# Gate and value of a SwiGLU block as one 2x2 block product by seven block multiplications, after thresholded attention

## The chip, the cores and the metric

The kernel runs on one core of one Trainium2 chip. The metric is the device time of one execution in microseconds (us). Work is spread over five engines with instruction streams of their own: TensorE (PE, matrix products; its weight loads are listed as PEld), VectorE (DVE), ScalarE (ACT), GpSimd (POOL) and SyncE (SP, which here only issues DMAs). Matrix products go to PSUM, which has 8 banks of 512 float32 columns on each of 128 partitions.

## What is computed

Eight batches with eight heads of 576 tokens and 64 channels each go through an attention that keeps only scores close to the row's maximum; then all 4608 rows of 512 channels go through a SwiGLU block of width 1536. Everything is float32 (the three weight matrices arrive as float64).

```python
def _attn_ref(q, k, v, tau):
    scale = 1.0 / np.sqrt(q.shape[-1])
    scores = scale * np.matmul(q, k.transpose(0, 1, 3, 2))
    thresh = np.max(scores, axis=-1, keepdims=True) - tau
    scores = np.where(scores >= thresh, scores, -1000000000.0)
    scores = scores - np.max(scores, axis=-1, keepdims=True)
    attn = np.exp(scores)
    attn = attn / (np.sum(attn, axis=-1, keepdims=True) + 1e-09)
    return np.matmul(attn, v)

def _moe_ref(x, w_gate, w_val, w_out):        # x: 4608 x 512
    g = x @ w_gate                            # 512 x 1536
    silu = g * (1.0 / (1.0 + np.exp(-g)))
    val = x @ w_val
    return silu * val @ w_out                 # 1536 x 512
```

## The kernel before

All of it is one instruction stream for each engine, in the order in which the Python code emits the instructions; each engine works its own list off strictly, and waits on the others where data demand it.

**Attention.** Work goes by segments: a pair of heads of one batch. A segment is cut into tiles of query tokens, four of 128 and one of 64 (`NT`); one such tile is a *slot*, so a batch is a block of 20 slots. Batch 0 is treated in a way of its own and is not touched in substance. From batch 1 on (`halved`), a slot runs so: PE writes two score tiles of two PSUM banks each (L345; one in the slot of 64 tokens; `ps_s` has two such tiles in all), DVE takes row maxima (`mx`, L368), exchanges them between partition groups (L318) and combines them (`nm`, L372), ACT computes the threshold (`th`, L383) and four exponentials into `pall` (L387), DVE masks and sums each (L391), ACT exchanges the sums (L321), DVE adds and inverts them (L406, L407), ACT and POOL scale two of the four pieces each (L399, L397), and DVE transposes them (L436). `turn(1)` leaves the newest scaled pieces lying, so that a transposition is emitted two slots after its scores. When the five slots of a segment are done, `attend` multiplies with `v` (L511) and ACT copies the result (`xa`) into the token buffer `xall` (L521, L528). The two arenas of `pall` in which successive segments put their exponentials overlap by two rows.

**SwiGLU.** Rows go through in units of 256 tokens: two of the first 512 tokens of each batch, and two that collect the last 64 tokens of four batches each, 18 in all. For each of 12 groups of 128 hidden columns, `rows_of_products` (L547) accumulates four products into `pg` (gate) and four into `pv` (value). ACT takes tanh and half of the gate (L560, L561), DVE and POOL make silu times value (L567, L579). The output product of the first two units is plain (L613); for the others `seven` (L645) treats it as a 2x2 block product (token halves by hidden halves times output halves) with seven block products instead of eight, with sums of weights (`ws2` to `ws4`) and of hidden blocks (`hs2`, `hs3`) made by POOL.

**Order.** PE interleaves both parts. `block()` is a generator that yields one matmul of the SwiGLU part at a time, and `fill(n)` draws n of them; `pace` sets how many each slot receives, so that the work left is spread evenly over the slots to come. In a slot come the scores, half of the share, the other half, and, in the second slot of a segment, the previous segment's `attend`. What is left after the last slot runs at the end with nothing beside it. q, k and v loads are issued on SP, output stores on POOL and at the end on SP.

Of the kernel before, what the change touches and what calls it, by code (L numbers as in the profile page):

```python
# [17 lines left out]

@with_exitstack
def kernel(  # L20
# [11 lines left out]

# [17 lines left out]
    XB = 5  # L68
# [7 lines left out]
    assert 2 * D == P and NCC == NP and D == 2 * G and S - SM == 2 * G and SM % TC == 0 and B % BT == 0 and QA == TC  # L76

    const = ctx.enter_context(tc.tile_pool(name="const", bufs=1))
    ld = ctx.enter_context(tc.tile_pool(name="ld", bufs=1))
    qkp = ctx.enter_context(tc.tile_pool(name="qkp", bufs=2))  # L80
    stp = ctx.enter_context(tc.tile_pool(name="stp", bufs=4))
    hp = ctx.enter_context(tc.tile_pool(name="hp", bufs=8))
    gp = ctx.enter_context(tc.tile_pool(name="gp", bufs=4))
    tp_ = ctx.enter_context(tc.tile_pool(name="tp", bufs=2))
    op = ctx.enter_context(tc.tile_pool(name="op", bufs=1))
    ps_s = ctx.enter_context(tc.tile_pool(name="ps_s", bufs=2, space=bass.MemoryType.PSUM))
    ps_f = ctx.enter_context(tc.tile_pool(name="ps_f", bufs=4, space=bass.MemoryType.PSUM))
    ctx.enter_context(tc.manual_schedule())


# [12 lines left out]
    vall = const.tile([P, 2 * NJ * D], F32, name="vall")  # L103


    NR = 2 * NT + 1
    pall = const.tile([P, 2 * NR - 2, S], F32, name="pall")

    free = NP * (S - TA * P)
    ident = pall.rearrange("p n s -> p (n s)")[:, free:free + P]  # L110
    make_identity(nc, ident)
    arenas = [pall[:, 0:NR, :], pall[:, NR - 2:, :]]

    ones = pall[:, 2 * NR - 4, 0:TC]
    nc.vector.memset(ones, 1.0)

    def run_idle(n):
        ps = ps_f.tile([P, 512], F32, name="idle", tag="psf")[:, 0:TC]
        for _ in range(n):
            nc.tensor.matmul(ps, ones[:, 0:P], ones, start=True, stop=True)  # L120

    wgv = const.tile([P, 2, NCC, DFF], F32, name="wgv")

    wo = const.tile([P, 2, NF, DM2], F32, name="wo")
# [4 lines left out]

    XW, HW = NCC * TC, NF2 * P  # L130
    xall = const.tile([P, XB * XW + 2 * HW], F32, name="xall")
    hs2, hs3 = (xall[:, XB * XW + n * HW:XB * XW + (n + 1) * HW].rearrange("p (f q) -> p f q", q=P)
                for n in range(2))


    extra = const.tile([P, 3 * NF2 * DM2], F32, name="extra")
    hfirst = extra[:, 0:NF * TC].rearrange("p (f n) -> p f n", n=TC)
    ws2, ws3, ws4 = (extra[:, n * NF2 * DM2:(n + 1) * NF2 * DM2].rearrange("p (f e) -> p f e", e=DM2)
                     for n in range(3))

# [4 lines left out]
    places += [xall[:, 3 * XW + n * 2 * TW:3 * XW + (n + 1) * 2 * TW] for n in range(2)]  # L156
    los = deque(extra[:, NF * TC + n * TW:NF * TC + (n + 1) * TW] for n in range(2))

    los.append(op.tile([P, 2, DM], F32, name="ob").rearrange("p i n -> p (i n)")[:, 0:TW])
# [66 lines left out]

    def load_qk(i):
        b, hp_ = divmod(i, NP)
        tiles = {}

        places_ = {1: extra[:, 0:2 * S], 2: extra[:, 2 * S:4 * S], 3: xall[:, XB * XW:XB * XW + 2 * S]}
        srcs = {"q": (q, "(j r) (e d) -> e r j d"),
                "k": (k, "(j r) (e d) -> e r j d" if b == 0 else "(r j) (e d) -> e r j d")}
        for x, name in enumerate("qk"):  # L240
            if i in places_:
                tiles[name] = places_[i][:, x * S:(x + 1) * S].rearrange("p (j d) -> p j d", d=G)
            else:
                tiles[name] = ld.tile([P, NJ, G], F32, name=f"{name}raw")
        raws = [tiles[name].rearrange("p j d -> p (j d)") for name in "qk"]
# [12 lines left out]
        if i < NP:  # L258

# [15 lines left out]

            own = xall[:, XB * XW + 2 * S:XB * XW + 3 * S - QA] if i == 0 else raws[0][:, QA:S]
# [7 lines left out]
        else:  # L284
            for name in "qk":
                load(name, slice(0, NJ), [nc.sync] * 2)
            if i == NP:
                scales.append(lambda: scale(raws[0]))
            else:
                scale(raws[0])  # L290
# [26 lines left out]
    def largest(out, in_):  # L317
        nc.vector.tensor_reduce(out=out, in_=in_, axis=AX.X, op=ALU.max)  # L318
# [665 lines left out]
```

## Time and profile before

| | us |
|---|---|
| three runs | 1507.58, 1509.18, 1509.38 |
| their median | 1509.18 |
| span of the profiled execution | 1509.0 |
| DVE busy in it | 997.8 |
| ACT busy | 726.6 |
| POOL busy | 642.1 |
| matmuls of gate, L547 `pg` (1728 records, two a matmul) | 403.9 |
| matmuls of value, L547 `pv` (1728 records) | 405.7 |
| matmuls of output, L645 (1344 records in three groups) | 311.5 |
| scores, L345 (4032 records) | 158.0 |
| attended product, L511 (2016 records) | 128.7 |
| POOL scaling, L397 | 265.4 |

The profile is of one execution. Busy time is the time in which at least one instruction of a group ran; matmuls overlap each other, so the price of one is read from the distance of their starts. A row of the timeline has the start, the duration up to the end of the last instruction of the row, the engine, the line, the operation with output and inputs, how many instructions are merged in it, and in brackets the idle time before it and what ended it. The mean clock granted to TensorE was 0.997 of full speed. DMA moved 66.93 MB, mean 44 GB/s.

### The profile page before, as it was taken

What the parts mean: (1) busy time and instruction counts of PE and PEld (TensorE: products, weight loads), DVE (VectorE), ACT (ScalarE), POOL (GpSimd) and SP (SyncE); (2) the same over time, 40 slices, a digit from 0 to 9 for tenths busy, and PEclk for the clock granted to TensorE, in tenths of its full rate; (3) what the DMA queues carried; (4) which work ended last, traced back from release to release, by engine and by line L of the source; (5) the groups of instructions that cost most, each with busy time, mean ns of one, the idle gap of its engine ahead of it and who ended that gap; (6) DMA issues with size and microseconds to landing.
All of it is one profiled execution on the core that took longest, in us unless ns stands there. A gap on an engine that the chain in (4) does not pass through costs nothing. (4 is left out here: it accounts for less than half of the span.)

```text
span 1509.0 us, 31516 instructions
## 1 busy us (share of the span) xinstructions
PE 1484.0 (98%) x11808; PEld 1124.8 (75%) x11808; DVE 997.8 (66%) x3040; ACT 726.6 (48%) x2158; POOL 642.1 (43%) x640
## 2 busy tenths in 40 slices
PE   9999899999999999999999999999999999999998
PEld 6677564477777777787777777777777777888887
DVE  7888887877777777737677666677666767412212
ACT  6887655555544545434545445454544554311110
POOL 2565543366453545435444444444545353500000
PEclk9999999999999999999999999999999999999999
DMA  7743211211111111112111011212110120000000
GB/s 176 194 152 88 69 33 43 50 33 33 46 33 47 33 43 23 39 22 46 33 40 21 20 46 33 46 33 47 33 43 11 40 48 16 1 14 1 15 15 14
DMA packets 177064, 66.93 MB, mean 44 GB/s; under 512 B 159888, under 2 KB 159888, under 8 KB 176912
## 3 DMA queue, kind: packets, MB, share of 16 engines
q1 hardware_dynamic: 170880, 56.62, 16.5%
q0 software_dynamic: 2432, 7.87, 1.4%
q8 instruction: 94, 1.54, 0.4%
q10 hardware_dynamic: 3600, 0.43, 0.2%
q14 instruction: 58, 0.48, 0.1%
HBM read 55.44 MB, written 9.44 MB: 43 GB/s over the span
## 5 line engine op out<-in xcount | busy, mean ns | idle before, releaser
L397 POOL TENSOR_SCALAR pall<-pall,ri 128x288 f32<-128x288 f32 (+1 forms) x260 | 265.4, 1030 | 345.3 <-DVE ri L407 328.2
L547 PE MATMUL pv<-xall,wgv 128*128 128x256 f32 x1728 | 405.7, 383 | 3.6 <-ACT pall L465 3.6
L547 PE MATMUL pg<-xall,wgv 128*128 128x256 f32 x1728 | 403.9, 383 | 0.7 <-ACT pall L465 0.7
L547 PEld LDWEIGHTS pv<-xall,wgv 128*128 128x128 f32 x1728 | 324.6, 190 | 69.3 <-issue 22.3
L547 PEld LDWEIGHTS pg<-xall,wgv 128*128 128x128 f32 x1728 | 324.1, 190 | 66.3 <-issue 22.0
L368 DVE TENSOR_REDUCE mx<-sc 128x2 f32<-128x576 f32 x252 | 180.7, 750 | 239.5 <-PE sc L345 238.5
L391 DVE SCALAR_TENSOR_TENSOR pall<-sc,th,pall 128x288 f32<-128x288 f32 (+1 forms) x540 | 258.0, 528 | 27.6 <-ACT pall L387 27.6
L387 ACT ACTIVATE pall<-sc,nm 128x288 f32<-128x288 f32 (+1 forms) x540 | 236.5, 510 | 0.6
L383 ACT ACTIVATE th<-nm,cut 128x4 f32<-128x4 f32 (+1 forms) x140 | 41.6, 297 | 386.1 <-DVE nm L372 386.1
L579 POOL TENSOR_TENSOR ht<-ht,gt 128x512 f32<-128x512 f32 x84 | 107.0, 1274 | 191.6 <-DVE ht L567 107.4
L436 DVE STREAM_TRANSPOSE pall<-pall 128x576 f32<-128x576 f32 x252 | 181.3, 754 | 2.8 <-POOL pall L397 2.8
L645 PE MATMUL po<-wo,ht 128*128 128x256 f32 x768 | 177.5, 381 | 0.0
L345 PE MATMUL sc<-kT,qT 64*32 64x288 f32 x4032 | 158.0, 411 | 12.2 <-DVE pall L391 10.9
L645 PEld LDWEIGHTS po<-wo,ht 128*128 128x128 f32 x768 | 144.6, 190 | 26.4 <-issue 6.0
L567 DVE SCALAR_TENSOR_TENSOR ht<-tn,pv 128x512 f32<-128x512 f32 x102 | 69.9, 685 | 132.3 <-PE pv L547 119.1
L399 ACT ACTIVATE pall<-pall,ri 128x288 f32<-128x288 f32 (+1 forms) x264 | 132.8, 553 | 0.0
L321 ACT COPY sums<-sums 32x4 f32<-32x4 f32 (+1 forms) x560 | 108.4, 194 | 50.0 <-DVE pall L391 38.8
L560 ACT ACTIVATE tn<-pg 128x512 f32<-128x512 f32 x108 | 64.8, 600 | 139.8 <-PE pg L547 133.0
L511 PE MATMUL xa<-pall,vall 64*64 64x288 f32 x2016 | 128.7, 405 | 0.0
L345 PEld LDWEIGHTS sc<-kT,qT 64*32 64x32 f32 x4032 | 58.8, 105 | 89.5 <-issue 60.9
L511 PEld LDWEIGHTS xa<-pall,vall 64*64 64x64 f32 x2016 | 74.3, 133 | 50.7 <-ACT sums L321 3.6
L663 POOL TENSOR_TENSOR ht<-ht,xall 128x256 f32<-128x256 f32 x48 | 34.1, 729 | 156.3 <-PE po L645 155.1
(114 smaller groups left out, 1336.5 us busy)
## 6 DMA issues: line engine op xcount, KB each, us to landing
vall<-in_v_dram SPq DMA_DIRECT2D x112, 144.0 KB, 3.4
kraw<-in_k_dram SPq DMA_DIRECT2D x114, 72.0 KB, 2.7
qraw<-in_q_dram SPq DMA_DIRECT2D x112, 72.0 KB, 2.4
out_dram<-ob POOLq DMA_DIRECT2D x28, 256.0 KB, 2.6
wo<-in_moe_w_gate_dram SPq DMA_DIRECT2D x16, 384.0 KB, 3.8
wo<-in_moe_w_val_dram SPq DMA_DIRECT2D x16, 384.0 KB, 4.4
xall<-in_moe_w_out_dram SPq DMA_DIRECT2D x5, 768.0 KB, 5.1
wo<-in_moe_w_out_dram SPq DMA_DIRECT2D x3, 768.0 KB, 6.3
```

The costliest lines, as they stand in the source:

```text
L321: nc.scalar.copy(out, in_[:, :, 0])
L345: nc.tensor.matmul(ps[g * G:(g + 1) * G, h, 0:SH], qT[hs, col + a * G:col + (a + 1) * G], kT[hs, c * SH:(c + 1) * SH], start=True, stop=True)
L368: nc.vector.tensor_reduce(out=mx[:, 2 * x:2 * x + 2, 0], in_=tile_[:, :, 0:SH], axis=AX.X, op=ALU.max, negate=True)
L387: nc.scalar.activation(ps[x], scs[x], AF.Exp, bias=nm[:, x:x + 1])
L391: nc.vector.scalar_tensor_tensor(out=ps[x], in0=scs[x], scalar=th[:, x:x + 1], in1=ps[x], op0=ALU.is_ge, op1=ALU.mult, accum_out=sm[:, x, ...
L397: nc.gpsimd.tensor_scalar(out=ps[x], in0=ps[x], scalar1=ri[:, x:x + 1], scalar2=None, op0=ALU.mult)
L399: nc.scalar.activation(ps[x], ps[x], AF.Copy, scale=ri[:, x:x + 1])
L436: nc.vector.transpose(out=p, in_=p)
L511: nc.tensor.matmul(xa[a][h * D:(h + 1) * D, at:at + n * G].rearrange("d (i q) -> d i q", q=G), vr[rs, h, j, :], p[rs, lo:lo + n, j, :], st ...
L547: nc.tensor.matmul(ps[:, i], wgv[:, mat, c, (f + i) * P:(f + i + 1) * P], x[:, c, cs], start=(c == 0), stop=(c == NCC - 1))
L579: eng.tensor_tensor(out=hts[x], in0=hts[x], in1=gt, op=ALU.mult)
L645: nc.tensor.matmul(ps, h(f), w[:, f, :], start=(f == 0), stop=(f == NF2 - 1))
```

## The change

**The product.** Gate and value of 512 tokens are taken as one block product. The token matrix is cut into two halves of 256 tokens by two halves of 256 channels, x11, x12, x21, x22; the weights for one group of 256 hidden columns into w11 (value, first channels), w12 (gate, first), w21 (value, second), w22 (gate, second). With

- s1 = x21 + x22, s2 = s1 - x11, s4 = x12 - s2, s3 = x11 - x21
- t1 = w12 - w11, t2 = w22 - t1, t4 = w21 - t2, t3 = w22 - w12

the seven products are p1 = x11 w11, p2 = x12 w21, p5 = s1 t1, p6 = s2 t2, p3 = s4 w22, p7 = s3 t3 and p4 = x22 t4, and value and gate of both halves are sums of these. Each is four matmuls of 256 columns (two groups of 128 hidden columns by two of 128 channels). A group of 256 hidden columns thus takes 28 matmuls in place of 32, and there are six such groups (`Group(c, g)`).

- Where two products are summed, PE writes the later one on into the same PSUM bank. Where a sum is used twice, ACT copies the bank in between (`cb`, `s5`, `u1`, `u2`); p2 waits for the copy of p1, p7 for that of p6, p4 for that of p7, p3 for that of p5. Gate sums are finished by DVE (`g1`) and POOL (`g2`).
- The sums of weights t1, t2, t4 are made once by POOL in block 1 and stored in DRAM (`sums_hbm`); `ring` holds two groups of them, and each group of each chunk is loaded again (`load_sums`, 768 KB, on SP) after p4 of two groups before. t3 takes the place of w12 in `wgv`. Slot 0 of the ring also serves as `hs2` and `hs3` of the output, so that its next load follows the fifth output product of a chunk's second half.
- Chunk 0 (batch 0) stays plain. Chunks 1 to 7 are the first 512 tokens of the other batches, chunk 8 collects the last 64 tokens of all batches, which go through DRAM (`last_hbm`).
- Four PSUM banks are handed out by name (`take`, `Hold`); at the end, when no scores run, four more.

**The order.** From batch 1 on, PE's order is a fixed table. Slots are numbered kk = 0 to 19 in a block; `GV` says how many of the 41 products of gate and value (the last p4 comes in slot 16) and `CH` how many of the 14 output products follow the scores of a slot. The table holds for blocks 2 to 7; in block 1 the plain work is shared out. `attend` of the previous segment comes in the third slot of a segment (kk = 2, 7, 12, 17), right behind the scores, ahead of the slot's other work.

The other engines' order follows from `Plan`: each piece of work is a `Job` with an engine, an estimated duration, a rank and what it depends on; when PE's next piece is emitted, all jobs that by the estimate have begun by then are emitted, for each engine the ready one of lowest rank first. A transposition (rank 2) is emitted when its scaled pieces are estimated to be ready, now one instruction of 1152 columns for a slot, where two of 576 were. Output stores go to SP.

In the built program, the exponentials of the slot with `attend` stand behind four ACT copies of `attend`'s result (L1210, L1211), and they write a part of `pall` that `attend` reads. DVE's transposition of a slot stands in most slots between `nm` and the first mask of the next slot.

```diff
+class Plan:
+    def job(self, eng, took, fn, *deps, rank=1, lag=0.0):
...
+                    n = min((i for i, j in enumerate(jobs) if j.ready <= start), key=lambda i: (jobs[i].rank, jobs[i].ready, i))
...
+    def pe(self, took, fn, *deps):
+        self.force(*deps)
+        for d in deps:
+            if d is not None:
+                self.t = max(self.t, (d.end if isinstance(d, Job) else d) + self.HOP)
+        self.run(self.t)
+        fn()
+        self.t += took
+        return self.t + self.PIPE
...
-            for f in range(0, NF, GR):
-                if f == EARLY:
-                    yield from late
-                yield from gate(j, cs, f, hts, gts)
-                if f >= EARLY:
-                    next(sums, 0)
-                yield from value(j, cs, f, hts, gts)
...
+    def weight_sums(g, s, *deps):
+        t1, t2, t4 = (ring_part(s, n) for n in range(3))
+        w11, w12, w21, w22 = pair_cols(wval, 0, g), pair_cols(wgat, 0, g), pair_cols(wval, 1, g), pair_cols(wgat, 1, g)
+        j = job("POOL", 1.3, pool_tt(t1, w12, w11, ALU.subtract), *deps, rank=3)
+        j = job("POOL", 1.3, pool_tt(t2, w22, t1, ALU.subtract), j, rank=3)
+        j = job("POOL", 1.3, pool_tt(t4, w21, t2, ALU.subtract), j, rank=3)
+        stores[g] = job("SP", 0.1, lambda: nc.sync.dma_start(out=sums_hbm[g], in_=ring[:, s]), j, lag=4.0)
...
+        def mul(self, hold, w, x, first, *deps):
+            def fn():
+                ps = hold.rows()
+                for i in range(2):
+                    for k_ in range(2):
+                        nc.tensor.matmul(ps[:, i], w[:, k_, i * P:(i + 1) * P], x[:, k_, :], start=first and i == k_ == 0,
+                                         stop=True, skip_group_check=True)
+            return pe(4 * MM, fn, *deps)
...
+        def p5(self):
+            m = self.mul(self.e, self.ring_w(0), xs[0], True, loads[self.c, self.g], ready_x[self.c][1], *self.e.deps)
...
+            self.s5 = job("ACT", 0.55, lambda: nc.scalar.activation(s.ap, self.e.rows(), AF.Copy, scale=0.5), m, *old, rank=0)
...
+        def p7(self):
+            m = self.mul(self.b, pair_cols(wgat, 0, self.g), x_block(self.c, 1, 0), False, self.u1, ready_x[self.c][3])
+            u, old = turn_of(u_bufs)
+            self.u2_buf = u
+            self.u2 = job("ACT", 0.55, lambda: nc.scalar.activation(u.ap, self.b.rows(), AF.Copy, scale=0.5), m, *old, rank=0)
+            tt, eng, took = (dve_tt, "DVE", 0.62) if tail[0] else (pool_tt, "POOL", 1.3)
+            self.g2 = job(eng, took, tt(u.ap, u.ap, self.s.ap, ALU.add), self.u2, self.s5, rank=1)
...
+        def p4(self):
+            m = self.mul(self.b, self.ring_w(2), x_block(self.c, 1, 1), False, self.u2)
+            self.finish(1, self.u2_buf, self.g2, self.b, m)
+            if self.g + 2 < NF2:
+                load_sums(self.c, self.g + 2, m)
...
+        for a in range(R):
+            def copy(a=a):
+                nc.scalar.copy(xk[:, a], holds[a].ap()[:, lo:lo + 2 * NT * G].rearrange("p (t i q) -> p t i q", t=2, q=G))
+                nc.scalar.copy(xl[:, a], holds[a].ap()[:, at_last:at_last + G])
+            js.append(job("ACT", 0.65, copy, m, last_store[0] if cc == 0 else None, rank=0))
...
+        seg["turned"].append(job("DVE", 0.72 * len(pss), lambda: nc.vector.transpose(out=whole, in_=whole), *scaled, rank=2))
...
+            new.p1(tail[0] or g in (0, 1, 3, 5))
+            yield
+            if old is not None:
+                old.p4()
+                yield
+            for fn in (new.p5, new.p2, new.p6, new.p3, new.p7):
+                fn()
+                yield
...
+    GV = {3: 4, 4: 3, 5: 4, 6: 4, 7: 1, 8: 4, 9: 2, 10: 4, 11: 3, 12: 1, 13: 4, 14: 3, 15: 4}
+    CH = {17: 1, 18: 3, 19: 2, 0: 3, 1: 2, 2: 1}
+    SHARES = [4.0, 4.0, 1.4, 4.0, 3.0]
...
+            pss, marks = slot_scores(seg, t)
...
+            if x == 2 and n > 0:
+                after = attend(halved[n - 1])
+                prepare_v(seg, after)
...
+            slot_rest(seg, t, pss, marks, after)
```

## The prediction

> **What bounds the kernel now.** I read the page's busy shares first, then busy time by stretches, then TensorE's timeline at the end, then all engines in one attention slot, then the DMA table. The share of each engine, and two stretches (columns: busy us and instructions of PE, PEld, DVE, ACT, POOL, then granted clock, DMA share, GB/s):
>
> ```profile
> PE 1484.0 (98%) x11808; PEld 1124.8 (75%) x11808; DVE 997.8 (66%) x3040; ACT 726.6 (48%) x2158; POOL 642.1 (43%) x640
> ```
>
> ```profile
> 180.00:190.00 10.00, 9.70 (x76) 6.88 (x77) 8.22 (x29) 5.85 (x18) 4.18 (x4) 0.83 0.41 88
> ...
> 420.00:580.00 160.00, 160.00 (x1380) 121.58 (x1383) 118.39 (x388) 82.33 (x260) 78.51 (x82) 1.00 0.17 38
> ```
>
> PE is busy without a gap from about 300 us on; DVE 74% and POOL 49% in the second stretch. So PE work that is removed comes out of the span one for one, until another wait opens. The price of that work is read at the end, where nothing else runs on PE (two records for each matmul):
>
> ```profile
> 1340.11 3.62 PE L547 MATMUL pg<-xall,wgv 128*128 128x256 f32 x16
> 1343.57 3.62 PE L547 MATMUL pv<-xall,wgv 128*128 128x256 f32 x16
> 1347.02 3.62 PE L547 MATMUL pg<-xall,wgv 128*128 128x256 f32 x16
> ```
>
> Groups of 16 records, 8 matmuls, start 3.453 us apart: 0.4316 us a matmul.
>
> Next the lags inside one attention slot:
>
> ```profile
> 803.81 4.59 PE L511 MATMUL xa<-pall,vall 64*64 64x288 f32 x72
> ...
> 808.34 1.20 PE L345 MATMUL sc<-kT,qT 64*32 64x288 f32 x32
> 808.44 0.77 ACT L521 COPY xall<-xa 128x128 f32<-128x128 f32 x4 [3.95 <-PE xa L511]
> 809.07 0.56 ACT L528 COPY xall<-xa 64x32 f32<-64x32 f32 x4
> 809.16 1.42 DVE L368 TENSOR_REDUCE mx<-sc 128x2 f32<-128x576 f32 x2 [6.12 <-PE sc L345]
> ...
> 811.65 1.43 DVE L436 STREAM_TRANSPOSE pall<-pall 128x576 f32<-128x576 f32 x2
> ```
>
> ```profile
> 799.70 1.65 ACT L387 ACTIVATE pall<-sc,nm 128x288 f32<-128x288 f32 x4
> ...
> 800.61 0.52 DVE L391 SCALAR_TENSOR_TENSOR pall<-sc,th,pall 128x288 f32<-128x288 f32 x1 [0.52 <-ACT pall L387]
> 801.05 0.08 DVE L391 DVE_READ_ACCUMULATOR pall<-sc,th,pall 128x1 f32 x1
> 801.05 0.51 DVE L391 SCALAR_TENSOR_TENSOR pall<-sc,th,pall 128x288 f32<-128x288 f32 x1
> ```
>
> ```profile
> 248.37 0.51 DVE L391 SCALAR_TENSOR_TENSOR pall<-sc,th,pall 128x288 f32<-128x288 f32 x1
> ...
> 249.04 0.72 PE L345 MATMUL sc<-kT,qT 64*32 64x288 f32 x16 [0.34 <-DVE pall L391]
> ```
>
> To be read: the two score units of a slot take PE 1.13 us (808.34 to 809.47, where the next matmul starts), one alone 0.57. The attended product takes 4.53 and its first copy starts at once (0.1 us after). Exponentials follow each other every 0.41 us; the first mask starts 0.91 us after the first exponential, further masks every 0.44 us. A freed score tile lets PE start 0.16 us after the mask's end (248.88 to 249.04).
>
> **What is removed.** Counted in the built programs: gate and value fall from 1728 matmuls of 256 columns to 192 plain (chunk 0) and 8 x 168 = 1344. That is 192 fewer, at 0.4316: -82.9 us. All other PE work keeps its counts (2016 score, 1008 attended, 672 + 48 output matmuls). Nothing hides it on PE, so it is worth its full price.
>
> **What is added, off PE.** For each chunk: 4 sums of tokens and 6 sums of gates on POOL (1.27 us each by the row L579, 1274 ns at the same shape), 12.7 us; 6 additions from PSUM on DVE (685 ns by L567), 4.1 us; on ACT 6 x 6 = 36 PSUM passes of 600 ns (rows L560, L561) for 24 before, +7.2 us. A block of 20 slots holds 42 x 1.726 (gate and value) + 84 x 0.4316 (output) + 36 x 0.57 + 4 x 4.53 = 147 us of PE work. POOL goes from 78 us in 160 to some 89 in 147 (61%), DVE to about 122 (83%), both beside PE: nothing by the sum. Weight sums (24 on POOL, six of these sets shipped out) lie in block 1 beside its plain work. The 48 reloads of weight sums, 768 KB each, are new SP issues; the same size now takes
>
> ```profile
> xall<-in_moe_w_out_dram SPq DMA_DIRECT2D x5, 768.0 KB, 5.1
> wo<-in_moe_w_out_dram SPq DMA_DIRECT2D x3, 768.0 KB, 6.3
> ```
>
> from issue to landing. A reload is issued when `p4` of a group ends and needed seven products later, 7 x 1.726 = 12.1 us, so it is hidden with 5.8 us to spare; queued ahead of it on SP are at most the eight q/k or four v loads of a slot. Only where the ring's slot 0 served as `hs2`, `hs3` is it close: two output products and one gate product, 6.9 us, in the two tail chunks. 0 to 2 us each; I take 1.0 each, 2 us.
>
> **What the new order costs PE.** This is the large unknown. The order of the built program shows three places (slots are numbered as in the table of the change).
>
> (1) The slot with `attend` (3rd of five). Its exponentials write where the attended product still reads, so they must wait for its end, T; and on ACT four copies stand ahead of them. Estimate from the rows: copies of 256 and of 32 columns issue about 0.29 + 0.14 us, twice: exponentials start at T + 0.95, masks at T + 1.86, the second mask ends at T + 2.81, PE may write that tile at T + 2.97. But the table gives PE only one product (1.73 us) after `attend` in slots 7 and 12, and one output product (2.59) in slots 2 and 17. PE stands 1.24 and 0.38 us. The second unit waits for the fourth mask, delayed by a PSUM pass of 0.5 us in slots 7 and 12 (T + 4.29) or an addition of 0.42 us (T + 4.27): another 0.75 and 0.73. So 2 x 1.99 + 2 x 1.11 = 6.2 us a block, 37 us in the six blocks 2 to 7. Before, the product stood at a slot's end, ahead of no exponential. Lower bound: first units alone, 3.2 a block, 19 us.
>
> (2) Slot 9 has one unit and two products, 4.1 us. Its masks come, by the same lags (reduction, exchange, 1.43 us transposition behind POOL's scaling, a PSUM pass among the exponentials), 4.5 to 6.6 us after its scores began, and slot 10's second unit needs them at 4.7. 0 to 1.9 us; I take 1.0: 6 us in six blocks (0 to 11).
>
> (3) Inside a group, PE writes on into a bank that ACT must first read. In 5 places of a chunk one product, 1.73 us, lies between; ACT needs 0.3 (lag of 1329.75 to 1330.01) + 0.6 and a lag back, 0.2 to 0.4. Hidden unless ACT is behind an exponential (0.41). 30 places at 0 to 0.4, I take 0.1: 3 us (0 to 12).
>
> Block 1 has the same `attend` waits, 4 x 1.2 = 5 us (0 to 10, since its neighbour work is plain and its idle time of before, 14 us between 150 and 290 us, may be there or not).
>
> [...] The largest wait for a score tile of before, 3.24 us, ended at 180.30; the clock of that stretch was 0.83. [...] By the row the waits above, 2 us at most, leave the clock at 1.00 and add nothing. [...]
>
> **The sum**, against the profiled execution's span of 1509.0 us (the median of the runs is 1509.18, so the span stands for the time): 1509.0 - 82.9 + 37 + 6 + 3 + 5 + 2 = 1479 us. With all low bounds 1509.0 - 82.9 + 19 = 1445; with all high ones 1509.0 - 82.9 + 37 + 11 + 12 + 10 + 4 = 1500.
>
> **Rivals.** (A) PE stays full. For it: 160.00 of 160 in the stretch above with the same kinds of waits, and DVE and POOL have room. Against it: the exponentials behind `attend`, which no spare engine time removes. 1426 + 5 to 10 for block 1 and the tail: 1434.
>
> (B) Slower: the loop through POOL sets the slot. Before, the transposition of a slot came two slots later; now most stand ahead of the next slot's masks, so mask, exchange, sum, scaling on POOL, transposition, mask closes a ring: 0.1 + 0.85 (L321) + 0.1 + 0.35 (L406, L407) + 0.1 + 1.98 (L397, two) + 0.05 + 1.43 + 1.82 (four masks) = 6.8 us, in slots of one unit 4.2. A block's ring is 16 x 6.8 + 4 x 4.2 = 126 us, 21 below PE's 147. A gating sum of 1.27 us ahead in every slot adds 25: 151. From about 1.7 us per slot on (160 a block, 13 x 6 = 78 and block 1) it eats the gain; at 1.9 us, 164 a block: 1426 + 6 x 17 = 1528. For it: POOL at 61% in strict order, and longer jobs among the scalings. Against: the mean wait would have to be one and a half sums in every slot.
>
> (C) The reloads come late, behind q/k loads of small packets: if each of the 36 reloads in the blocks landed one us beyond the 5.8 spare, that would be 36 us on top of the forecast, 1515. The spare grows by the score and attended work between, so it is unlikely.
>
> That the products are not fewer is excluded by the count.
>
> **How the numbers follow.** Forecast (waits of this size, 1455 to 1500): 0.62, time 1479. (A) 0.18. (B) 0.09, (C) 0.02, both slower. The rest, 0.09, lies between 1500 and 1512: 0.06 faster, 0.03 unchanged, which here means within 0.2%, 3 us. Faster 0.62 + 0.18 + 0.06 = 0.86, same 0.03, slower 0.11. The range reaches from the low bounds, taking in half of (A), to 1508: 1440 to 1508.
>
> **What would show it.** Right: `sc` waits on DVE masks at the slot after `attend`, 1 to 2 us each, some 24 times, PE busy 95 to 97% in the middle, no gap of PE over 2.5 us, clock 1.00; 0.43 us a matmul in the products. Wrong upwards: DVE waiting for POOL at the transposition in most slots; `pe` waiting for a DMA. Wrong downwards: PE at 160 of 160 again.

## The result and the profile after

The changed kernel takes 1585.7 us (median of 4 runs, 1584.3 to 1591.3), the kernel before 1508.5 us beside it: ratio 1.052, 95% interval 1.050 to 1.054. It is slower by 77 us where 30 us less had been forecast, and the time lies outside the range. The profiled execution has a span of 1583.0 us at a mean clock of 0.970.

The page of the changed kernel, shares of the engines and two rows of the span in 40 slices (one slice is 39.6 us):

```profile
PE 1444.0 (91%) x11424; PEld 1059.8 (67%) x11424; DVE 1070.9 (68%) x3032; ACT 799.2 (50%) x2142; POOL 699.9 (44%) x661
...
PE   9998665767999999999999999999999999999998
...
PEclk9999778789999999999999999999999999999999
```

PE has the 384 records (192 matmuls) less that were counted, and still stands 139 us instead of 25. The second line says where: in slices 4 to 9 (counted from 0, about 160 to 400 us) PE is 50 to 80% busy, and in all but the last of them the third line shows a lower clock. From slice 10 on both are high again. Two stretches of the changed kernel (columns: busy us and instructions of PE, PEld, DVE, ACT, POOL, then granted clock, DMA share, GB/s):

```profile
160.00:200.00 40.00, 23.22 (x152) 14.82 (x150) 23.49 (x71) 16.61 (x44) 12.92 (x12) 0.74 0.11 20
400.00:1340.00 940.00, 898.70 (x7948) 659.67 (x7941) 726.77 (x2205) 543.21 (x1547) 517.22 (x517) 1.00 0.26 66
```

In the first, no engine is full: 58% of PE, 59% of DVE, 32% of POOL. That is the mark of a chain in which each engine waits for another, at a clock of 0.74. The second is blocks 2 to 7: PE stands 41.3 us of 940, close to the 46 us that the forecast has there (37 + 6 + 3).

It pays to cut the span at one event that all these kernels have, the first matmul of the block product of chunk 1 (in the kernel before, the first matmul of its chunk 1). Ahead of it lie the start and block 1, the first batch with halved attention, beside which chunk 0's plain products run.

| us | before | after | difference | forecast |
|---|---|---|---|---|
| up to the first product of chunk 1 | 298.4 | 400.1 | +101.7 | +5 |
| from there to the end | 1210.6 | 1182.9 | -27.7 | -35 |
| span | 1509.0 | 1583.0 | +74.0 | -30 |

So the loss is in block 1 alone. From 150 us on, PE stood 82 us there (250 less 167.9) where it had stood 12 (150 less 137.8), and its matmuls took 30 us longer for nearly the same work (columns as above, the kernel before and then the changed one):

```profile
150.00:300.00 150.00, 137.79 (x1241) 77.54 (x1226) 123.26 (x403) 86.41 (x278) 61.36 (x57) 0.99 0.21 49
...
150.00:400.00 250.00, 167.88 (x1282) 88.53 (x1282) 133.56 (x410) 92.13 (x273) 108.77 (x96) 0.81 0.19 54
```

What PE waited for in 160 to 400 us of the changed kernel (us in total, times, longest):

```profile
PE sc L1111 <- DVE pall L1148: 79.6, 27, 6.6
...
POOL hall L517 <- DVE hall L510: 46.1, 7, 11.0
DVE hall L510 <- PE pv L486: 37.3, 7, 7.7
```

PE's scores (L1111) wait for the masks (L1148) that free the score tile, 2.9 us each in the mean. The third line points to the cause, seen from DVE: it stands 37 us for a plain value matmul (`pv`), work that has nothing to do with the scores. One slot of the changed kernel shows the circle (start, duration, engine, line, operation, records, idle time before and what ended it):

```profile
176.06 2.18 PE L1111 MATMUL sc<-kT,qT 64*32 64x288 f32 x32 [4.50 <-DVE pall L1148]
...
178.17 5.13 PE L486 MATMUL pv<-xall,wgv 128*128 128x256 f32 x16
...
183.14 1.89 PE L486 MATMUL pg<-xall,wgv 128*128 128x256 f32 x8
183.34 0.69 DVE L510 SCALAR_TENSOR_TENSOR hall<-tmp,pv 128x512 f32<-128x512 f32 x1 [4.49 <-PE pv L486]
183.94 0.75 DVE L1133 TENSOR_REDUCE mx<-sc 128x2 f32<-128x576 f32 x1
184.17 1.26 POOL L517 TENSOR_TENSOR hall<-hall,tmp 128x512 f32<-128x512 f32 x1 [3.37 <-DVE hall L510]
...
185.41 1.98 POOL L1175 TENSOR_SCALAR pall<-pall,ri 128x288 f32<-128x288 f32 x2
...
187.42 1.38 DVE L1179 STREAM_TRANSPOSE pall<-pall 128x1152 f32<-128x1152 f32 x1 [0.93 <-POOL pall L1175]
...
189.80 1.22 PE L1111 MATMUL sc<-kT,qT 64*32 64x288 f32 x16 [4.77 <-DVE pall L1148]
```

The first scores of this slot are there at about 177.1 us, and DVE is free from 178.9 on. But ahead of their maxima (L1133) its list has the gated value of a plain product (L510), and that waits until the slot's value matmuls are done: 183.34. So the maxima start 5 us late, POOL multiplies the gate (L517) before it scales the pieces of the slot before (L1175), the transposition (L1179) waits for that, the masks come behind it, and PE has long finished the slot's plain work when the score tile comes free: it stands 4.77 us. In 160 to 400 us DVE stands so seven times (the third line above), and ACT ten times in the same way for a plain gate or output product, 39.4 us in all. Then the clock: the two score units at 176.06 took 2.11 us to the next matmul's start instead of 1.13, and the eight plain matmuls behind them 4.97 instead of 3.45.

Why the order is so: `plain(n)` draws the plain matmuls by `fill(n)`, which emits each matmul's readers at once (tanh and half gate on ACT, gated value on DVE, gate on POOL, output copy on ACT, store on POOL), while the slot's softmax is jobs of the plan, emitted only as the next `pe()` runs the plan. All of the slot's plain matmuls and readers thus stand ahead of the slot's maxima in every list. This is in the built program: in block 1's slots `hall<-tmp,pv` stands before the maxima on DVE.

The waits of blocks 2 to 7 in the changed kernel's timeline, one `attend` (its matmuls run from 753.08 to 757.7 us) and the slots behind it:

```profile
758.22 1.99 PE L867 MATMUL pe<-xall,ring 128*128 128x256 f32 x8 [0.55 <-ACT xlast L1211]
760.64 0.72 PE L1111 MATMUL sc<-kT,qT 64*32 64x288 f32 x16 [0.42 <-DVE pall L1148]
762.17 0.72 PE L1111 MATMUL sc<-kT,qT 64*32 64x288 f32 x16 [0.81 <-DVE pall L1148]
...
775.67 0.72 PE L1111 MATMUL sc<-kT,qT 64*32 64x288 f32 x16 [0.73 <-DVE pall L1148]
```

These are the places of steps (1) and (2): 1.23 us for the two units behind an `attend` where 1.99 was forecast, 0.73 ahead of slot 10 where 1.0 was. A wait that the forecast lacks, 0.55 us for ACT's copy of `attend`'s result, and some others of 0.3 to 0.7 make up for it. Step (3) does not show: in 400 to 1340 us PE waits for no copy inside a group. And the reloads of the weight sums, in the changed kernel's table of DMA issues (times, KB each, median us from issue to landing):

```profile
ring<-sums_hbm SPq DMA_DIRECT2D x48, 768.0 KB, 4.3
```

PE never waits for them.

### The profile page after: what moved, and what is told of

It is laid out like the page before. It is cut to its first block, busy times and chain, and to the rows that moved or that the text cites. A ratio compares the mean times of both kernels' runs of the same rounds, so it can differ in the third digit from the quotient of the medians.

```text
span 1583.0 us, 30968 instructions
## 1 busy us (share of the span) xinstructions
PE 1444.0 (91%) x11424; PEld 1059.8 (67%) x11424; DVE 1070.9 (68%) x3032; ACT 799.2 (50%) x2142; POOL 699.9 (44%) x661
## 4 chain that ended last, share of the span: by engine, by line
PE 70%; DVE 13%; ACT 6%; issue 3%; SPq 3%; DMA 3%; POOL 2%; DVEq 0%; ACTq 0%; POOLq 0%
PE po L995 16%; PE pb L867 14%; PE pa L867 10%; PE xa L1198 8%; PE pe L867 8%; PE sc L1111 8%; DVE pall L1148 4%; ACT pall L1147 2%; SPq L305 2%; PE pv L486 2%; PE po L539 2%; DVE pall L1179 2%; DMA kT<-in_k_dram 1%; PE pg L486 1%; ACT xall L1210 1%
## 5 line engine op out<-in xcount | busy, mean ns | idle before, releaser
L1175 POOL TENSOR_SCALAR pall<-pall,ri 128x288 f32<-128x288 f32 x252 | 250.0, 1002 | 277.2 <-DVE ri L1168 262.3
L1148 DVE SCALAR_TENSOR_TENSOR pall<-sc,th,pall 128x288 f32<-128x288 f32 x504 | 240.2, 507 | 121.7 <-ACT pall L1147 120.1
L1111 PE MATMUL sc<-kT,qT 64*32 64x288 f32 x4032 | 179.1, 436 | 119.2 <-DVE pall L1148 117.8
L1147 ACT ACTIVATE pall<-sc,nm 128x288 f32<-128x288 f32 x504 | 227.4, 497 | 60.4 <-DVE pall L1148 57.7
L1179 DVE STREAM_TRANSPOSE pall<-pall 128x1152 f32<-128x1152 f32 (+1 forms) x140 | 175.8, 1256 | 60.2 <-POOL pall L1175 55.1
L1111 PEld LDWEIGHTS sc<-kT,qT 64*32 64x32 f32 x4032 | 55.7, 108 | 215.7 <-issue 106.6
L1133 DVE TENSOR_REDUCE mx<-sc 128x2 f32<-128x576 f32 x252 | 182.6, 747 | 17.8 <-PE sc L1111 16.9
L867 PE MATMUL pa<-xall,wgv 128*128 128x256 f32 x768 | 186.6, 386 | 0.0
L867 PE MATMUL pb<-xall,ring 128*128 128x256 f32 x768 | 182.1, 380 | 0.0
L995 PE MATMUL po<-wo,hall 128*128 128x256 f32 x768 | 176.6, 382 | 0.3 <-DVE ob L1014 0.3
L1178 ACT ACTIVATE pall<-pall,ri 128x288 f32<-128x288 f32 x252 | 123.0, 528 | 95.6 <-DVE ri L1168 94.9
L867 PEld LDWEIGHTS pa<-xall,wgv 128*128 128x128 f32 x768 | 144.0, 191 | 35.5 <-issue 13.5
L995 PEld LDWEIGHTS po<-wo,hall 128*128 128x128 f32 x768 | 144.0, 190 | 29.7 <-issue 7.2
L867 PEld LDWEIGHTS pb<-xall,ring 128*128 128x128 f32 x768 | 145.5, 190 | 22.3 <-ACT pb L877 2.8
```

The lines of the kernel that those rows point to most:

```text
L867: nc.tensor.matmul(ps[:, i], w[:, k_, i * P:(i + 1) * P], x[:, k_, :], start=first and i == k_ == 0, stop=True, skip_group_check=True)
L995: nc.tensor.matmul(ps, h(f), w[:, f, :], start=(f == 0), stop=(f == NF2 - 1))
L1111: nc.tensor.matmul(ps[g * G:(g + 1) * G, h, 0:SH], qT[hs, col:col + G], kT[hs, c * SH:(c + 1) * SH], start=True, stop=True)
L1133: rs.append(job("DVE", 0.72, lambda x=x, tile_=tile_: nc.vector.tensor_reduce(out=mx[:, 2 * x:2 * x + 2, 0], in_=tile_[:, :, 0:SH], axis=A ...
L1147: ej = job("ACT", 0.42, lambda x=x: nc.scalar.activation(ps[x], scs[x], AF.Exp, bias=nm[:, x:x + 1]), ej, after, rank=0)
L1148: mj = job("DVE", 0.45, lambda x=x: nc.vector.scalar_tensor_tensor(out=ps[x], in0=scs[x], scalar=th[:, x:x + 1], in1=ps[x], op0=ALU.is_ge, ...
```

## The experiments

Four theories. Q: the readers of chunk 0's plain work stand ahead of the slot's softmax in the engines' lists. P: POOL has too much work in block 1 (six sets of weight sums are new there). M: exponentials on ACT and masks on DVE take turns at a PSUM tile, so that the chain of a slot is longer than the plan thinks. L, later: the plan's estimate of the q and k loads is wrong, and their users are placed too early. Times are medians, with the ratio to the kernel before on the same chip and its 95% interval; "first product" is the cut of the table above. In the texts recorded before the runs, theory L is called D once (8), "rival L" in 4 is another one (a ring through POOL sets the pace), and "the first one" and "the third one" are 1 and 3, but in 8 "the third one" is 7.

**1. The plan run after each plain matmul.** It lets softmax jobs come between plain matmuls, but their readers are still emitted at once.

```diff
-        done = fill(n)
-        plan.t += done * MM
+        while n > 0:
+            done = fill(min(n, 1))
+            plan.t += done * MM
+            plan.run(plan.t)
+            n -= 1
```

> In block 1 the plan is also run after every plain matmul, so that the softmax jobs of the slot come to stand ahead of the readers of the plain products on DVE, ACT and POOL. Nothing else is changed. Theory Q (order of queues: PE waits since DVE and ACT first wait for the slot's last plain product and only then start the slot's softmax): block 1, from its first scores to the first product of chunk 1, falls from 252 us to about 155 (149 before), the whole to about 1485 us (1470 to 1505), and the clock stays at 0.99 or more. Rival P (POOL: 24 weight sums and 9 output sums of 1.27 us each stand in block 1): block 1 stays above 220 us, the whole above 1550. Rival C (the clock alone, which fell to 0.74): no change of the waits of 4 to 6 us, 1575 or more.

1539.3 us, 1.019 (1.016 to 1.022); first product at 353.7 us. 46 of the 77 us are back, all of them in block 1, so the order within the slots does count. It falls well short of what was expected.

**2. POOL's new work doubled.** Each set of stored weight sums is made twice in block 1, some 23 us more of POOL.

```diff
-        j = job("POOL", 1.3, pool_tt(t1, w12, w11, ALU.subtract), *deps, rank=3)
...
+        for _ in range(2):
+            j = job("POOL", 1.3, pool_tt(t1, w12, w11, ALU.subtract), *deps, rank=3)
...
+            deps = (j,)
```

> The changed kernel with each of the 18 sums of weights that are stored made twice on POOL, 18 x 1.27 = 23 us more work for POOL in block 1; the results are the same. Rival P: each sum delays the scaling behind it, so the time rises by 20 us or more over 1586. Theory Q: POOL mostly has time while the slot waits for its plain product; the rise is under 12 us.

1586.1 us, 1.051 (1.049 to 1.053): nothing, though POOL's busy time in 150 to 400 us rose from 108.8 to 131.3 us. P falls; POOL waits for others in block 1.

**3. As 1, and chunk 0's output stores on SyncE instead of POOL.**

```diff
-                    send(unit, i, nc.gpsimd)
+                    send(unit, i, nc.sync)
```

> As the first one, and the four output stores of chunk 0 are issued on SP rather than on POOL, where they wait up to 11 us for ACT's copy with scalings queued behind. Theory Q extended to POOL: 2 to 15 us less than the first one. If the stores cost nothing there: within 2 us of it.

1542.8 us, 1.022 (1.021 to 1.024): no gain over 1. POOL's wait for the output copy ahead of a store is not on the path.

**4. As 3, and `attend` ahead of the third slot's scores,** with a table that puts more work between them and the next scores (`GV` 1 and 4 in slots 6 and 7, 1 and 3 in slots 11 and 12, the same in `CH` and the shares).

```diff
+            after = None
+            if x == 2 and n > 0:
+                after = attend(halved[n - 1])
+                prepare_v(seg, after)
             pss, marks = slot_scores(seg, t)
-            after = None
...
-            if x == 2 and n > 0:
-                after = attend(halved[n - 1])
-                prepare_v(seg, after)
```

> As the third one, and the attended product is put ahead of the scores of a segment's third slot instead of behind them, with the table of products moved along (GV 6: 1, 7: 4, 11: 1, 12: 3; CH 17: 2, 18: 2, 1: 1, 2: 2; shares likewise). Theory A of the forecast (exponentials behind the attended product cost about 6 us of PE in each of blocks 2 to 7): the waits of scores in the slot after it vanish, 20 to 40 us less than the third one, about 1450. Rival L (the ring mask, exchange, POOL scaling, transposition, mask sets the pace of a block, whatever the place): less than 8 us gained, the waits appear in other slots.

1523.7 us, 1.010 (1.009 to 1.012): 19 us less than 3, about the least that was expected. But the first product comes at 333.4 us instead of 353.4, and the time from there on is 1187.8 instead of 1185.4: the gain is block 1's. In blocks 2 to 7, where the edit was to take away the 37 us behind `attend`, it brought nothing. Why not is shown in 9 to 11.

**5. Pairing alone, on the changed kernel:** both masks of a score tile wait for both of its exponentials.

```diff
+            exps.append(ej)
+        for x in range(m):
...
-                ej, *old_sums, rank=0)
+                exps[x | 1], *old_sums, rank=0)
```

> The changed kernel with one edit: the two masks of a score tile are made to depend on both exponentials of that tile, so that ACT's list has both ahead of the first mask again. Seen in the changed kernel: the second exponential of a tile waits for the first mask (58 us of such waits in all), which never occurs before; from the first exponential to the last mask it is 3.9 us where it was 2.7. Theory M (accesses of ACT and DVE to one score tile are serialised, and the alternating order lengthens every slot's chain by about 1 us): 20 to 35 us less than 1586, half of it in block 1. Rival: the alternation only fills time in which the chain waits for something else: less than 6 us.

1594.1 us, 1.056 (1.054 to 1.058): 8 us more. The turns are real, and pairing ends them. All waits of this kind in the changed kernel:

```profile
DVE pall L1148 <- ACT pall L1147: 120.1, 143, 4.3
...
ACT pall L1147 <- DVE pall L1148: 57.7, 92, 2.6
```

and in the kernel with pairing, where exponentials (now L1148) no longer wait for masks (now L1151):

```profile
DVE pall L1151 <- ACT pall L1148: 93.5, 55, 4.4
```

Yet the time grew, so theory M falls as a cause of the loss: taking 58 us of waits off ACT gained nothing. Pairing also makes the first mask of a tile wait for a second exponential, so what the turns alone cost is not shown.

**6. Theory Q in full:** as 1, and each reader of chunk 0 a job of the plan with what it depends on (tanh, half gate, gated value, gate, output copy, store; a bank's next user waits for its readers; stores on SyncE).

```diff
-        nc.vector.scalar_tensor_tensor(out=ht, in0=tn, scalar=1.0, in1=ps, op0=ALU.add, op1=ALU.mult)
+            vj = job("DVE", 0.7, lambda: nc.vector.scalar_tensor_tensor(out=ht, in0=tn, scalar=1.0, in1=ps, op0=ALU.add, op1=ALU.mult),
+                     ended(), tj, rank=1)
+            reader(whole, vj)
...
+            mj = job("POOL", 1.3, lambda: nc.gpsimd.tensor_tensor(out=ht, in0=ht, in1=gt, op=ALU.mult), vj, gj, rank=1)
```

> The changed kernel, the plan run after every plain matmul, and besides the readers of chunk 0's plain products in block 1 (tanh, half gate, gated value, product of both, output copies and stores) handed to the plan as jobs with their dependences, so that none stands ahead of work that is ready earlier by the estimate. Theory Q in full (the readers' places in the in-order lists are the whole of block 1's loss): block 1 at most 175 us, total at most 1512. Rival Q-part (the readers are half of it, the rest is the slot's own chain, which is longer than the 6.4 us of PE work that a slot of block 1 has): block 1 at 190 to 205, total 1525 to 1542, as in the run with the plan between.

1512.2 us, 1.0015 (1.0005 to 1.0024): 73.5 us less, just outside what Q foresaw (block 1 at 178 us where 175 was the most, 1512.2 where 1512 was). The first product comes at 326.2 us, some 178 us after the first scores of block 1; from there on the time is unchanged (1184.2 against 1182.9). The same part of block 1 in this kernel (scores are L1149, masks L1186, maxima L1171, the gated value L534, the transposition L1217):

```profile
180.32 1.38 DVE L1217 STREAM_TRANSPOSE pall<-pall 128x1152 f32<-128x1152 f32 x1 [1.49 <-POOL pall L1213]
...
182.87 0.71 PE L1149 MATMUL sc<-kT,qT 64*32 64x288 f32 x16
...
183.34 0.68 DVE L534 SCALAR_TENSOR_TENSOR hall<-tmp,pv 128x512 f32<-128x512 f32 x1
...
183.94 0.75 DVE L1171 TENSOR_REDUCE mx<-sc 128x2 f32<-128x576 f32 x1
...
187.17 0.71 PE L1149 MATMUL sc<-kT,qT 64*32 64x288 f32 x16
```

The gated value now runs right behind the masks without a wait on DVE, the maxima 0.6 us behind it, and the two score units shown start without a wait and take 0.71 us. PE's waits for masks in block 1 fall from 84.1 us in 29 to 30.1 in 22. Q is shown: of the 102 us that block 1 lost, 74 came from the order of these readers. The other 28 stayed: the kernel before waited 10.9 us there.

**7. As 6, with `attend` ahead (4) and the pairing (5).**

> The attended product ahead of the scores, both exponentials ahead of the masks, and readers planned, all three. Theory M with theory Q-part: the gains add, 1523.7 less 20 to 40: 1485 to 1505, below the kernel before. If the chain is bound elsewhere (POOL's scaling and the transposition): above 1512.

1493.6 us, 0.990 (0.989 to 0.992). Most of the gain over 6 is again block 1's (first product at 312.4 us); from there 1179.5. The time lies in the range of theory M with Q-part, but not for M's reason: 10 takes the pairing out again and loses nothing.

**8. As 7, with a measured price for the loads.** The plan thought that a unit's eight q and k loads take 0.8 us of SyncE; in the trace four of q take about 2 us to issue and four of k about 2.6.

```diff
-        fj = job("SP", 0.8, fetch, later_than, lag=3.5)
+        fj = job("SP", 4.6, fetch, later_than, lag=2.7)
```

> As the third one, and the estimate of the q and k loads set to what the trace shows (SP issues the eight in 4.65 us, the last lands 2.7 us later; the plan had 0.8 and 3.5). Theory D (the transposition of k and the scaling of q stand too early in the lists of DVE and POOL and wait there for the DMA, 9 us and 29 us in the changed kernel): 4 to 12 us less than the third one. Rival: these waits are hidden, within 2 us.

1467.1 us, 0.972 (0.970 to 0.973): 26 us less, far more than expected, and this time from the first product on (1153.7 us). The estimate moves no load (SyncE's 538 issues stand in the same order in both kernels); it moves what stands behind the loads. In the kernel of 6, POOL's scaling of q (L1275) and DVE's transposition of k (L1277) wait for data (in that of 7 the same pair waits 15.2 and 24.3 us):

```profile
POOL qT L1275 <- DMA qT<-in_q_dram: 31.3, 10, 4.3
...
DVE kT L1277 <- DMA kT<-in_k_dram: 12.7, 12, 2.1
```

With the measured price both lines are gone.

**9. As 6, with the measured loads alone.**

> The kernel with chunk 0's readers as planned jobs (1512.2 us), and one number more: the plan takes 4.6 us of SyncE and 2.7 us of lag for the eight q and k loads of a unit instead of 0.8 and 3.5, as the trace shows them; `attend` stays behind the third slot's scores. Theory L (the table places the scaling on POOL and the transpositions on DVE before their data has landed, so both lists stand still 3 to 5 us a unit): 1482 to 1498 us, the 26 us that the same edit brought once `attend` was ahead. Rival (the loads count only where the scores of a unit follow at once, which `attend` ahead brings about): 1505 to 1512 us.

1507.0 us, 1.000 (0.998 to 1.001): 5 us, though the waits of the two lines above are gone here as well. The rival is right.

**10. As 8, without the pairing.**

> The fastest kernel so far (1467.1 us) without the pairing, so that each mask waits for its own exponential again. Theory M (each exponential after the first waits for the mask before it, as ACT and DVE take turns at one PSUM tile, which lengthens the chain of a slot): 1470 to 1480 us. Rival (pairing only delays the first mask, as its +8 us alone suggests): 1456 to 1464 us.

1463.5 us, 0.970 (0.969 to 0.972): 4 us less, in the range of the rival, though the two intervals overlap. Pairing gains nothing. This is the fastest kernel of the study, 46 us below the kernel before.

**11. As 10, with the old price of the loads.** It closes a square.

> The fastest kernel so far (1463.5 us: chunk 0's readers planned, `attend` ahead of the third slot's scores, measured loads) with the old estimate of the loads (0.8 and 3.5 us); it closes a square with 1512.2 (neither), 1507.0 (measured loads alone). If the two edits are worth the same each way (5 us for the loads, 43 to 49 for `attend` ahead): 1464 to 1471 us. If the loads' estimate counts only once `attend` is ahead (26 us between the two kernels with pairing, which then does nothing to it): 1485 to 1495 us.

1506.0 us, 0.998 (0.997 to 0.999), above both ranges, so the two edits work only together, even more than was expected:

| us | old price of the loads | measured price |
|---|---|---|
| `attend` behind the scores | 1512.2 | 1507.0 |
| `attend` ahead of the scores | 1506.0 | 1463.5 |

Two waits take each other's place. With `attend` behind, the score tile is late in every third slot whatever the loads do: from the first product on, PE waits 34.3 us for masks by the old price and 35.0 by the measured one. With `attend` ahead, most of that wait is gone, but by the old price DVE and POOL stand for q and k (16.0 and 21.1 us in all, nothing by the measured one), and `attend`'s matmuls (L1236) meet a PSUM bank that an addition on DVE (L970) has not yet read. In this kernel, at 666 us, the addition and the matmuls that stand for it:

```profile
665.51 0.68 DVE L970 SCALAR_TENSOR_TENSOR tmp<-pe,tmp 128x512 f32<-128x512 f32 x1
...
666.25 7.24 PE L1236 MATMUL xa<-pall,vall 64*64 64x288 f32 x68 [3.26 <-DVE tmp L970]
```

It is the order of DVE's list that makes this addition late, and not the time lost for loads: in the 11 us ahead of each of these waits no engine waits for q or k. By the old price the list has the addition behind four masks at all six places, and the transposition of q (L1280) ahead of the maxima; by the measured price the addition stands right behind `nm`, ahead of these masks and of L1280. The waits for k are likely to cost something directly as well: in each of the six blocks a wait of PE for masks, 7.0 us in all, ends 1.7 to 1.8 us after one of them.

The six waits for the addition take 19.3 us, one a block, where the kernel of 10 has 7.9 us; waits for masks take 14.8 against 2.7; and the attended matmuls run 9.9 us longer in all (143.3 against 133.4 us): behind five of the six waits they took 6.0 to 7.2 us instead of 4.6, as matmuls did behind the waits of block 1. With 4.9 us more in the scores these make 38 of the 42 us between the two kernels from the first product on (1186.6 and 1144.5). PE's waits of the kernel of 10 from 316 us on:

```profile
PE xa L1236 <- DVE tmp L970: 7.9, 6, 1.3
PE sc L1149 <- DVE pall L1186: 2.7, 7, 0.5
```

**12. As 8, with one of the seven products issued twice,** the second overwriting the first: the 192 matmuls are back and no other engine has more to do.

```diff
-            self.m1 = self.mul(self.a, pair_cols(wval, 0, self.g), x_block(self.c, 0, 0), True, *self.a.deps)
+            for _ in range(2):
+                self.m1 = self.mul(self.a, pair_cols(wval, 0, self.g), x_block(self.c, 0, 0), True, *self.a.deps)
```

> The fastest kernel so far (1467.1 us) with one of the seven products of each group issued twice (the second overwrites the first), which puts the 192 removed matmuls back and leaves every other operation as it is. Step 'the removed products are worth 82.9 us' with TensorE as the bound: 1535 to 1550 us, at 0.38 to 0.43 us a matmul less at most some 15 us of waits that they fill (TensorE stands 17.6 us of the 939 us from the first product on). Rival (other engines set the slots even here, and the added matmuls lie in their waits): 1467 to 1500 us.

1535.5 us, 1.017 (1.016 to 1.019): 68.4 us more than 8. PE's busy time by groups (matmul records, busy us, mean ns of one, idle before), the first product's row of the kernel of 8:

```profile
L905 PE MATMUL pa<-xall,wgv 128*128 128x256 f32 x768 | 185.8, 385 | 0.0
```

and of this kernel:

```profile
L905 PE MATMUL pa<-xall,wgv 128*128 128x256 f32 x1152 | 268.8, 383 | 0.0
```

83.0 us for 192 matmuls, 0.432 each, the price that the forecast used. Of the 14.6 us that do not show in the span, 6.5 us went into waits of scores and attended matmuls (34.9 to 28.4 us), and scores and plain value matmuls ran 6.6 us shorter.

## Why the prediction was wrong, point by point

**The removed products: right.** -82.9 us was the forecast; putting them back adds 83.0 us of PE's time and 68.4 us to the span where the rest of the order is mended. In the changed kernel PE's busy time from the first product on fell by 70.3 us (1206.7 to 1136.4); scores took 8.3 us more of it (137.6 against 129.3 in blocks 2 to 7).

**Blocks 2 to 7: right in sum, less so in its parts.** 41.3 us of idle PE against 46. The waits lie where steps (1) and (2) have them, but they are shorter (60 waits for masks, 33.7 us, the longest 1.1 us, where "1 to 2 us each, some 24 times" was forecast) and there are more of them. Step (3), 3 us, did not show, and 6.6 us for ACT's copy of `attend`'s result were not foreseen. That the sum comes so close is in part luck.

**Tail and reloads: right.** PE stands 5.3 us in the last 243; no PE wait for the 48 reloads.

**Block 1: the step that failed.** The term was "the same `attend` waits, 4 x 1.2 = 5 us (0 to 10, since its neighbour work is plain ...)". It measured 102 us. (The idle time of before in 150 to 290 us, given there as 14 us, is 12.2.) The premise was that plain work is emitted as before and so behaves as before; but the work that it shares a slot with had become jobs of a plan, emitted later. The order of the built program showed the gated value ahead of the maxima in these slots, and the forecast looked only at blocks 2 to 7 for order. 74 of the 102 us are shown to be this order (experiment 6). The remaining 28 are partly the order around `attend` (the first product comes at 316.4 us in experiment 11); in the fastest kernel block 1 is still 18 us longer than before, with 22 us of waits for masks, and the cause of that stays open.

**The clock: a condition that the forecast left out of its sum.** It took waits of 2 us at most, which would leave the clock alone, as one of 2.60 us in the kernel before did (the scores behind it, at 164.82, took 0.72 us, at a granted clock of 1.00). In block 1, 13 waits were 4.1 to 6.6 us long, and the granted clock in 150 to 400 us was 0.81. All 13 were followed by slow scores: 1.04 to 1.22 us for one unit and 2.18 for two, where the kernel before took 0.72 and 1.20. The forecast has no price for such a wait in its sum. The slot shown took from 176.06 to 183.14, 7.08 us, for what takes 1.13 + 8 x 0.4316 = 4.58 by the prices measured in the kernel before, so 2.5 us. If each of the 13 costs that, 13 x 2.5 = 33 us (an estimate from one slot), which agrees with the 30 us by which PE's busy time in block 1 grew. The trace's record of the granted clock agrees too: from 150 to 403 us it is at 0.50 in 14 stretches, 95.6 us in all, 12 of them 6.8 us or longer. PE is busy in 68 us of that, so about 34 us are lost (an estimate: half of 68, by the clock of 0.50); the kernel before has one such stretch in block 1, 3.4 us.

**The rivals.** (A), PE stays full, did not come about; the kernel of 10 comes nearest, with 10.6 us of idle PE in blocks 2 to 7. (B), the loop of mask, exchange, POOL, transposition and mask, did set the slot, but in block 1, where plain work stood in the loop, and not in blocks 2 to 7 from POOL's load, as the rival had it; doubling POOL's weight sums cost nothing. (C), late reloads, did not occur.

## What to carry to other kernels

Where one part of a kernel is put under a planner and another still emits its readers at once, look at each engine's list in the stage in which both meet: an instruction that waits for the last matmul of a slot must not stand ahead of one that needs only the first. A stage that the change does not touch is to be costed anew if the work beside it is emitted in another way. If two waits can stand in for one another, taking away either shows almost nothing (6 and 5 us here, 49 together), so a fix without effect is not yet a cause ruled out; and a planner's estimates are best set from the trace, including what it costs to issue a load, since they set the order of every list: in the kernel of 11 a wrong price for loads put an addition for which PE stands behind four masks.

## What the hardware showed that was not expected

**How long a wait slows TensorE.** In block 1 of eight of these kernels (before, after, 1, 5, 6, 8, 10, 11), all 28 waits for masks of 4.1 us and more were followed by slow scores (1.04 to 1.22 us for one unit instead of 0.72, 2.2 for two instead of 1.2). Of the 18 waits between 2.5 and 4.02 us nine were, the shortest of 2.77 us, while one of 4.02 was not. So the length of a wait alone did not decide here. Waits of 3.26 us in the kernel of 11 show it best: the matmuls behind them (68 records of L1236) took 4.58 us at 506.35, 7.24 at 666.25 and 6.17 at 828.84.

The traces also record when the granted clock changed, between 1.00 and 0.50. In the changed kernel's the changes lie whole multiples of 3.41 us apart, wherever a wait begins. Cut into steps of 3.41 us at these points, up to the last matmul, it has 14 steps at 1.00 behind which the clock was 0.50; in them PE was busy, by the profile, for 0 to 1.22 us. Behind the other 418 steps at 1.00 it stayed, and PE was busy in each of them for 1.46 us or more. In the kernel before it fell behind two steps, with 0.17 and 1.41 us of PE's work, and stayed behind the 435 others, with 1.81 us or more. In these two traces the work left in such a step thus tells the cases apart.

**Issuing small loads.** Four q loads of a unit (72 KB each) kept SyncE's queue 2.1 us in the median of the changed kernel (1.9 to 3.2), four k loads 2.6 (up to 5.3). The plan had 0.8 us of SyncE for all eight, and 3.5 us for the landing, where the table of DMA issues has 2.5 and 2.7.

**ACT and DVE at one score tile.** A second exponential did not start while a mask read the same PSUM tile, though both only read it: in the changed kernel this came up at 123 of 252 tiles, and each time the exponential began only when the mask had ended, 0.04 us after it at the least; the waits are mostly 0.6 to 0.7 us. Whether the chip needs this or only the built program orders it so was not tried. Ending these turns by pairing gained nothing: 8 us more on the changed kernel, 4 us more at the end.
